# Expert 0's first product ahead of the routing, its rows from a slot table of twelve tiles, with a branch that does expert 0 again

## The chip, the core and the metric

The kernel runs on one core of a Trainium2 chip. The metric is the device time of one execution in microseconds (us). TensorE multiplies, VectorE and ScalarE work on vectors, GpSimd too (and it issues the gathers), SyncE issues most of the other transfers. In the profile they are PE (PEld is its loading of weights), DVE, ACT, POOL and SP.

## What is computed

Three stages in a row, each on 2304 tokens of 512 values; the last two have 8 experts with a hidden width of 1024.

```python
attn = softmax(q k^T / 8) v            # in chunks of 64 tokens, 8 heads of 64
# first mixture: one expert for each token, at most capacity = 576 tokens each
e = argmax(x @ w_gate);  g = softmax(x @ w_gate)[e]
out[i] = g[i] * relu(x[i] @ w1[e]) @ w2[e]       # by the order of the tokens in each expert
# second mixture: every expert for every token
P = exp(x @ w2_gate - max), 8 times: rows and columns divided by their sums, times N / E
out = sum over e of P[:, e] * relu(x @ w21[e]) @ w22[e]
```

The inputs are drawn from a fixed seed. Worked out with them, the reference sends 512, 128, 466, 384, 174, 128, 320 and 192 tokens to experts 0 to 7; of the first 1536 tokens (12 tiles of 128) 320 go to expert 0.

## The kernel before

A tile is 128 tokens; there are NT = 18. Numbers go as pairs of float16 (a high and a low part), so that a product is three matmuls: high by high, high by low, low by high.

**Attention and routing.** One loop over n (24 steps) runs the stages `st_...` of several tiles side by side, each with its lag, in the order written in `order`. `st_tr`, `st_dtr` and `st_xtr` transpose on TensorE through three PSUM banks (`ps_t`). The finished rows of a tile go to DRAM (`xs_d`) as a float16 pair by `st_hi` (ScalarE, L455) and `st_lo` (VectorE, L459, and the transfer). For each group of three tiles `route(g)` finds each token's expert and its place in it, and adds one product to a table in PSUM (`p_tab`, L570), from which `tacc` sums the table of slots: for expert e and slot s, the token's number (`gidx`, L577, after the last group). Expert 0's weights are loaded and split into pairs in the meantime. After the loop come the last group's steps, the table, and one matmul (L685) that counts the tokens of every expert, into the registers that branches and addresses read (`reg_i`, L686).

**The experts of the first mixture.** For expert x, GpSimd gathers rows of `xs_d` by the table (L712): slots 0 to 255 (`first`, for later experts `rows`) and 256 to 511 (`late`). Their transposes come from TensorE (`turn`) or from a transfer of SyncE (`turn_dma`, L721). The gathered tiles, like all tiles of this stage, take memory that the pools of the attention stage held until they were closed, behind the count. `blocks` does 256 tokens: a first product of four groups of 24 matmuls (L764), each followed by two vector steps (`hh` on ScalarE, L768; `hl` on VectorE, L769), then a second product of two times 24 (L781) with its scaling and two transfers. The first call is for everyone; if an expert has over 256 tokens, a second call on the `late` rows runs in a branch, for one or two tiles. Between the groups stand `sites`, the places where the next expert's weights are made ready: `w_scale`, then `w_split`, which makes the pairs. `behind`, after the first tile of the second product, holds the statistics (`w_stat`) of the expert after that: a sum of squares on ScalarE (L168) or a largest value on VectorE (L170). The loads go to SyncE in program order (L157).

**The rest.** The second mixture (from L910) is a long chain of products with every transfer planned by hand; the change doesn't touch it.

## Time and profile before

| | |
|---|---|
| median of 3 timed runs | 1789.73 us (1787.1 to 1792.47) |
| the profiled execution | 1782.29 us, of which the span of the profile is 1780.6 us |
| TensorE busy in the span | 1695.9 us (95%) |
| granted TensorE clock, mean | 0.985 of full speed |

The profile is that of one execution; its span runs from its first to its last record. A line of it gives the start in us from there, the duration, the engine, the line of the kernel, the operation and its operands, and in brackets how long the engine had been idle and what released it.

### The profile page before, as it was taken

The numbers are of one execution on the slowest core, as the hardware profiler recorded it, in microseconds if no ns is written. First come the engines' busy times: TensorE is split into PE (matmuls) and PEld (weight loads), VectorE is DVE, ScalarE is ACT, GpSimd is POOL, SyncE is SP. The second block draws the span as 40 slices with busy tenths as digits, with TensorE's granted clock in tenths as the row PEclk, the third lists the DMA queues.
The fourth block names the chain that finished last, engine by engine and source line by source line (L and its number), as shares of the span: only waits on it lengthen the run. The fifth ranks groups of instructions, "written<-read, shape, count | busy, mean of one in ns | idle before, by whom it ended". The sixth has DMA issues, their size and how long they took to land.

```text
span 1780.6 us, 32980 instructions
## 1 busy us (share of the span) xinstructions
PE 1695.9 (95%) x13011; PEld 1227.1 (69%) x13011; DVE 1202.5 (68%) x2340; ACT 954.4 (54%) x1806; POOL 731.8 (41%) x754
## 2 busy tenths in 40 slices
PE   7877999999999999999999999999999999999995
PEld 5765667566555577777777777777777777777774
DVE  4896556766476766686677767676866776675652
ACT  7965556675355454665355545455653664453440
POOL 1345335552021334444454344454533553443432
PEclk9997999999999999999999999999999999999998
DMA  9847678942534223241324224223323142231200
GB/s 240 211 155 214 148 199 178 247 127 85 145 102 147 89 105 130 64 168 53 124 83 152 104 91 151 104 84 110 138 77 131 63 172 87 86 125 65 96 36 36
DMA packets 140902, 219.15 MB, mean 123 GB/s; under 512 B 62880, under 2 KB 81392, under 8 KB 140720
## 3 DMA queue, kind: packets, MB, share of 16 engines
q1 hardware_dynamic: 133728, 198.92, 35.6%
q0 software_dynamic: 5360, 17.24, 3.5%
q8 instruction: 115, 1.88, 0.4%
q14 instruction: 67, 0.55, 0.1%
q10 hardware_dynamic: 1632, 0.56, 0.1%
HBM read 167.56 MB, written 41.91 MB: 118 GB/s over the span
## 4 chain that ended last, share of the span: by engine, by line
PE 68%; DVE 5%; ACT 2%; DMA 1%; issue 1%; POOLq 0%; ACTq 0%; DVEq 0%
PE p_m L1122 35%; PE p_m L1210 28%; PE p_m L1254 5%; DVE wall L290 3%; ACT wall L289 1%; DVE acc L1189 1%; DMA out_dram<-acc,rk 1%; DVE el L1130 0%; PE p_m L1010 0%; ACT eh L1127 0%; DMA wb_d<-wall 0%; DVE tq L1137 0%; ACT tq L1162 0%; DMA x_d<-row 0%; DVE tq L1140 0%
## 5 line engine op out<-in xcount | busy, mean ns | idle before, releaser
L1122 PE MATMUL p_m<-x,wall 128*128 128x384 f16 x4032 | 666.7, 326 | 5.6 <-ACT tq L1162 4.1
L1210 PE MATMUL p_m<-wall,eh 128*128 128x256 f16 x3528 | 580.4, 273 | 0.0
L1122 PEld LDWEIGHTS <-wall 128*128 128x128 f16 x4032 | 394.0, 98 | 263.0 <-issue 8.4
L1134 POOL TENSOR_TENSOR el<-tq,eh 128x384 f16<-128x384 f32 x336 | 344.4, 1053 | 558.9 <-ACT eh L1127 558.6
L1210 PE MATMUL p_m<-wall,el 128*128 128x256 f16 x1764 | 480.8, 273 | 0.3 <-DVE el L1130 0.3
L1127 ACT ACTIVATE eh<-tq 128x384 f16<-128x384 f32 x540 | 274.0, 522 | 190.6 <-DVE tq L1140 101.9
L1210 PEld LDWEIGHTS <-eh 128*128 128x128 f16 x3528 | 344.3, 98 | 44.3
L1189 DVE SCALAR_TENSOR_TENSOR acc<-p_m,cf,acc 128x256 f32<-128x256 f32 (+1 forms) x378 | 175.1, 521 | 128.0 <-PE p_m L1210 128.0
L1137 DVE TENSOR_TENSOR tq<-p_m,tq 128x384 f32<-128x384 f32 x288 | 158.5, 556 | 128.3 <-PE p_m L1122 127.3
L1210 PEld LDWEIGHTS <-el 128*128 128x128 f16 x1764 | 172.6, 98 | 20.5 <-DVE el L1130 0.6
L1130 DVE SCALAR_TENSOR_TENSOR el<-tq,eh 128x384 f16<-128x384 f32 x204 | 175.7, 863 | 10.0 <-ACT eh L1127 8.6
L1140 DVE SCALAR_TENSOR_TENSOR tq<-tq 128x384 f32<-128x384 f32 x252 | 133.2, 553 | 2.9
L764 PEld LDWEIGHTS <-wall 128*128 128x128 f16 x1152 | 106.5, 100 | 26.5 <-issue 10.2
L1162 ACT COPY tq<-p_m 128x384 f32<-128x384 f32 x96 | 45.6, 475 | 110.2 <-PE p_m L1122 107.8
L764 PE MATMUL p_p<-xT,wall 128*128 128x256 f16 x768 | 90.3, 279 | 7.5 <-DMA sta<-in_moe_w_dram 2.8
L1254 PE MATMUL p_m<-wall,eh 128*128 128x512 f16 x288 | 85.6, 379 | 0.0
L268 POOL TENSOR_TENSOR tq<-stb 128x256 f32<-128x256 f32 x56 | 48.9, 873 | 81.9 <-DVE wsumsq L184 58.9
L1175 ACT ACTIVATE tq<-tq 128x384 f32<-128x384 f32 x84 | 43.9, 523 | 70.1 <-DVE tq L1137 70.1
L289 ACT ACTIVATE wall<-stb,wsb 128x256 f16<-128x256 f32 (+1 forms) x56 | 31.3, 606 | 87.5 <-DMA wb_d<-wall 62.1
L268 POOL TENSOR_TENSOR tq<-sta 128x256 f32<-128x256 f32 x56 | 45.0, 804 | 72.9 <-DVE wall L290 43.4
L240 POOL TENSOR_SCALAR stb<-stb,wsb 128x1024 f32<-128x1024 f32 x16 | 53.7, 3358 | 46.7 <-DVE tq L1137 43.4
L290 DVE SCALAR_TENSOR_TENSOR wall<-stb,wsb,wall 128x256 f16<-128x256 f32 (+1 forms) x56 | 38.1, 690 | 51.4 <-ACT wall L289 48.7
(261 smaller groups left out, 2123.3 us busy)
## 6 DMA issues: line engine op xcount, KB each, us to landing
x<-xt_d SPq DMA_DIRECT2D x147, 384.0 KB, 3.6
sta<-in_moe_w_dram SPq DMA_DIRECT2D x18, 1024.0 KB, 6.7
stb<-in_moe_w_dram SPq DMA_DIRECT2D x18, 1024.0 KB, 9.0
wb_d<-wall SPq DMA_DIRECT2D x20, 896.0 KB, 3.6
wall<-wb_d SPq DMA_DIRECT2D x20, 896.0 KB, 6.3
sta<-in_moe_w_dram SPq DMA_DIRECT2D x28, 512.0 KB, 8.5
stb<-in_moe_w_dram SPq DMA_DIRECT2D x28, 512.0 KB, 6.3
xt_d<-x SPq DMA_DIRECT2D x21, 384.0 KB, 3.9
```

The costliest lines, as they stand in the source:

```text
L268: nc.gpsimd.tensor_tensor(out=at(o), in0=at(u), in1=at(v), op=op)
L290: nc.vector.scalar_tensor_tensor(out=o[:, cs, 1], in0=src, scalar=m.s, in1=o[:, cs, 0], op0=ALU.mult, op1=ALU.subtract)
L764: nc.tensor.matmul(p[:, f4, :], lhsT=w[:, kk, f * 128:(f + 1) * 128], rhs=xT[:, lo + kk, 0:W], start=(n == 0), stop=(n == 3 * KD - 1))
L1122: nc.tensor.matmul(p, lhsT=wt[:, w, lw, kk, :], rhs=xt[:, lx, kk, :], start=first and n == 0, stop=n == 5, skip_group_check=not first)
L1127: nc.scalar.activation(out=hs[op][0][:, q, :], in_=src, func=AF.Relu if op in (A11, A12, A22) or plain else AF.Copy)
L1130: nc.vector.scalar_tensor_tensor(out=hs[op][1][:, q, :], in0=src, scalar=0.0, in1=hs[op][0][:, q, :], op0=ALU.max, op1=ALU.subtract)
L1134: nc.gpsimd.tensor_tensor(out=hs[op][1][:, q, :], in0=src, in1=hs[op][0][:, q, :], op=ALU.subtract)
L1137: nc.vector.tensor_tensor(out=o, in0=a, in1=b, op=ALU.add)
L1140: nc.vector.scalar_tensor_tensor(out=o, in0=a, scalar=0.0, in1=b, op0=ALU.max, op1=op)
L1189: nc.vector.scalar_tensor_tensor(out=acc[:, j, cols], in0=y, scalar=coefs[x][:, j:j + 1], in1=acc[:, j, cols], op0=ALU.mult, op1=ALU.add)
L1210: nc.tensor.matmul(bk.t[:, cols], lhsT=hs[op][lh][:, q, t * 128:(t + 1) * 128], rhs=b.q[q][:, w, lw, :], start=m in (1, 5) and q == 0 and ...
L1254: nc.tensor.matmul(y.t, lhsT=h[:, kk % 4, c * 128:(c + 1) * 128], rhs=w[:, kk, :], start=(n == 0), stop=(n == 3 * KF - 1))
```

## The change

- **A slot table of twelve tiles.** The table of group 3 (tiles 9 to 11) is done in step 19 instead of 20 to 22 (`hooks`). From the sum over groups 0 to 3, VectorE takes expert 0's first 256 slots (`e_idx`), and GpSimd gathers those rows into the buffer of the weights (`wall`), which is free then. The number of expert 0's tokens in these tiles is kept in `e_count` a group later.
- **The first product of expert 0** moves into the end of the attention loop: the transposes after step 21 (`turn_into`), the groups of 24 matmuls after steps 22 and 23, after the last group's vector steps, and ahead of the count. The three transpose banks are shared with it.
- **Expert 1's statistics** are all sums of squares on ScalarE, three after step 22, three after step 23, two further on. Before, four were on VectorE.
- **Expert 1's splits of its first matrix** and the loads of expert 2 come ahead of expert 0's second product, the rest of the splits after its first tile. The transposes of the `late` rows come after both tiles.
- **The loads** of experts 2 and up are each preceded by a `memset` of one column on VectorE, on which the load then waits; from expert 1 on they are issued quarter by quarter in the sites.
- **A branch** behind expert 0: if the twelve tiles hold under 256 of its tokens, both tiles are done again from the whole table.

```diff
@@ -149,11 +149,13 @@
         m.src = src
         m.mx = smw("wmx" + nm, [128, 4])
 
-    def w_load(x, nm, h, nh=2):
+    def w_load(x, nm, h, nh=2, behind_vector=False):
         if h == 0:
             w_new(x, nm)
         m = mats[x, nm]
         c = m.kk // nh
+        if behind_vector:
+            nc.vector.memset(m.st[:, h * c, 0:1], 0.0)
         nc.sync.dma_start(out=m.st[:, h * c:(h + 1) * c, :],
                           in_=m.src[h * c * 128:(h + 1) * c * 128, :].rearrange("(k p) n -> p k n", p=128))
...
+    banks = {i: ctx.enter_context(tc.tile_pool(name="ps_a", bufs=1, space=PSUM)) for i in range(1)}
+    turns = {"p": [0, 1, 2], "y": [3, 4], "c": [5, 6]}
+
+    def bank_tile(i, shape, dtype, nm):
+        return banks[0 if i in (0, 1, 2) else 1].tile(shape, dtype, tag=f"m{i}", name=nm)
+
+    def in_turn(kind, shape, dtype, nm):
+        i = turns[kind].pop(0)
+        turns[kind].append(i)
+        return bank_tile(i, shape, dtype, nm)
+
+    early = wall[:, 2 * 4096:4 * 4096]
+    e_rows = [wall[:, t * 2 * XW:(t + 1) * 2 * XW].bitcast(F32) for t in range(2)]
+    e_hh, e_hl, e_xT = (early[:, i * 2048:(i + 1) * 2048].rearrange("p (k t) -> p k t", t=256) for i in range(3))
+    e_idx = const.tile([128, 2], I32, name="e_idx")
+    e_kg = const.tile([128, 2], F32, name="e_kg")
+    e_count = const.tile([128, 2], I32, name="e_count")
+    EG = NG - 3
+
+    def turn_into(xT, rows, bank):
+        for n, (idx, kg, xg) in enumerate(rows):
+            p = in_turn(bank, [128, 2 * KD, 128], F16, "p_t")
+            for kk in range(2 * KD):
+                nc.tensor.transpose(p[:, kk, :], xg[:, kk * 128:(kk + 1) * 128], id16)
+            sl = slice(n * 128, (n + 1) * 128)
+            nc.scalar.copy(out=xT[:, 0:KD, sl], in_=p[:, 0:KD])
+            nc.vector.tensor_copy(xT[:, KD:2 * KD, sl], p[:, KD:2 * KD])
+
+    def first_product(x, xT, hh, hl, W, bank):
+        a = mats[x, "a"]
+        FG = 512 // W
+        for fg in range(KF // FG):
+            p = bank([128, FG, W])
+            for f4 in range(FG):
+                f = fg * FG + f4
+                n = 0
+                for w, lo in ((a.hi, 0), (a.hi, KD), (a.lo, 0)):
+                    for kk in range(KD):
+                        nc.tensor.matmul(p[:, f4, :], lhsT=w[:, kk, f * 128:(f + 1) * 128], rhs=xT[:, lo + kk, 0:W],
+                                         start=(n == 0), stop=(n == 3 * KD - 1))
+                        n += 1
+
+            def hidden(fs=slice(fg * FG, fg * FG + FG), p=p):
+                nc.scalar.activation(out=hh[:, fs, :], in_=p, func=AF.Relu)
+                nc.vector.scalar_tensor_tensor(out=hl[:, fs, :], in0=p, scalar=0.0, in1=hh[:, fs, :],
+                                               op0=ALU.max, op1=ALU.subtract)
+
+            yield hidden
...
-                p = ps_t.tile([128, PR, 128], F32, tag="t", name="p_t")
+                p = in_turn("p", [128, PR, 128], F32, "p_t")
...
+        e_tokens = [(e_idx[:, j:j + 1], e_kg[:, j:j + 1], e_rows[j][:, 0:DM].bitcast(F16)) for j in range(2)]
+        e_first = first_product(0, e_xT, e_hh, e_hl, 256, lambda shape: in_turn("p", shape, F32, "p_p"))
+        hidden, hooks = [], {}
+        next_stats = [lambda nm=nm, h=h: w_stat(1, nm, h, True) for nm in "ab" for h in range(4)]
+
+        def early_gather():
+            nc.vector.tensor_copy(e_idx, tacc[:, 0:2])
+            for j in range(2):
+                nc.gpsimd.indirect_dma_start(out=e_rows[j], out_offset=None, in_=xs_d[0:(EG + 1) * G * 128, :],
+                                             in_offset=bass.IndirectOffsetOnAxis(ap=e_idx[:, j:j + 1], axis=0))
+
+        def counted():
+            nc.vector.tensor_copy(e_count, p_tab[:, 256:258])
+
         todo_r = {}
         for n in range(NT + 6):
             if n % 2 == 1 and n // 2 + 2 < NS:
@@ -650,8 +714,19 @@
                 for r in first + mm:
                     r()
             if i >= 0 and i % G == G - 1 and i < NT - G:
-                for m, part in zip((n, n + 1, n + 1, n + 3, n + 5), route(i // G)):
-                    todo_r.setdefault(m, []).append(part)
+                first_g, mm_g, mid_g, tab_g, last_g = route(i // G)
+                if i // G == EG:
+                    kept_g, sum_g, out_g = last_g
+                    hooks[n + 2, st_lo] = [kept_g, out_g]
+                    hooks[n + 2, st_scores] = tab_g
+                    hooks[n + 2, st_max] = [sum_g, early_gather]
+                else:
+                    todo_r.setdefault(n + 3, []).append(tab_g)
+                    todo_r.setdefault(n + 5, []).append(last_g)
+                if i // G == EG + 1:
+                    mid_g.append(counted)
+                todo_r.setdefault(n, []).append(first_g)
+                todo_r.setdefault(n + 1, []).extend((mm_g, mid_g))
...
+                for r in hooks.pop((n, f), ()):
+                    r()
...
+            if n == NT + 3:
+                turn_into(e_xT, e_tokens, "p")
+                for j in range(2):
+                    nc.vector.tensor_copy(e_kg[:, j:j + 1], e_rows[j][:, DM:DM + 1])
+            if n >= NT + 4:
+                hidden.append(next(e_first))
+                for f in next_stats[:3]:
+                    f()
+                next_stats = next_stats[3:]
         for n in sorted(todo_r):
             for part in todo_r[n]:
                 for r in part:
                     r()
-        for r in [gw, eps, rec, sel, pos, kx, rout, *second, *tab, tot1, tot2, racc]:
+        for r in [gw, eps, rec, sel, pos, kx, rout, *second]:
             r()
+        hidden.append(next(e_first))
+        hidden[0]()
+        for r in [*tab, tot1, tot2, racc]:
+            r()
+        next_stats[0]()
+        hidden[1]()
+        next_stats[1]()
+        hidden.append(next(e_first))
...
+        for f in hidden[2:]:
+            f()
...
+            if x == 0 and main:
+                hh, hl = e_hh, e_hl
+            else:
+                hh = cp.tile([128, KF, 256], F16, tag="hh", name="hh", bufs=1)[:, :, 0:W]
+                hl = cp.tile([128, KF, 256], F16, tag="hl", name="hl", bufs=1)[:, :, 0:W]
+                for hidden in first_product(x, xT, hh, hl, W, lambda shape: bank("p", shape)):
+                    hidden()
...
+        def load(x, nm, *hs):
+            return [lambda h=h: w_load(x, nm, h, 4, True) for h in hs]
...
-        first = gather(tokens(0, 0, 1))
+        pre = (None, e_tokens)
+
         late = gather(tokens(0, 2, 3))
         rows = gather(tokens(1, 0, 1))
-        for f in stats(1):
-            f()
-        pre = turn(first, "xT")
 
         for x in range(E):
             y = x + 1
-            rc = nc.values_load(reg_i[0:1, x:x + 1], min_val=0, max_val=N)
+
+            def count():
+                return nc.values_load(reg_i[0:1, x:x + 1], min_val=0, max_val=N)
+
+            if x > 0:
+                rc = count()
...
+            def rows_ahead():
+                return gather(tokens(y, 2, 3)) if y < E else None, gather(tokens(y + 1, 0, 1)) if y + 1 < E else None
+
             cur, pre = pre, turn_dma(rows) if y < E else None
-            late_cur, late = late, gather(tokens(y, 2, 3)) if y < E else None
-            rows = gather(tokens(y + 1, 0, 1)) if y + 1 < E else None
-            if x == 0:
-                for nm in "ab":
-                    loads(2, nm)
-            elif x + 2 < E:
-                loads(x + 2, "b", 0, 2)
+            late_cur = late
+            if x > 0:
+                late, rows = rows_ahead()
...
-                      ((0, "a"), (2, "b"), (1, "a"), (2, "a"), (3, "b"), (3, "a"), (0, "b"), (1, "b"))]
+                      (((0, "a"), (2, "b"), (1, "a"), (2, "a"), (3, "b"), (3, "a"), (0, "b"), (1, "b")) if x > 0 else
+                       ((0, "a"), (1, "a"), (2, "a"), (3, "a"), (2, "b"), (3, "b"), (0, "b"), (1, "b")))]
...
-            if 0 < x < E - 2:
-                sites[1].append(lambda: loads(x + 2, "b", 2, 4))
-            behind = [lambda: loads(x + 3, "a", 0, 2)] if x + 3 <= E else [lambda: loads(E, "b")] if x == E - 2 else []
+            later = load(x + 3, "a", 0, 1, 2, 3) if x + 3 <= E else load(E, "b", 0, 1, 2, 3) if x == E - 2 else []
+            behind = later[:1]
             for h in range(4):
                 if x + 2 <= E:
                     behind.append(lambda h=h: w_stat(x + 2, "a", h, True))
                 if x + 2 < E:
                     behind.append(lambda h=h: w_stat(x + 2, "b", h, False))
+                    if x > 0:
+                        sites[h] += load(x + 2, "b", h)
                 elif x == E - 1:
                     sites[h].append(lambda h=h: w_stat(E, "b", h, True))
-            sites += [behind, [lambda: loads(x + 3, "a", 2, 4)] if x + 3 <= E else []]
-            nxt = []
-            blocks(x, cur, 2, ranks(0), sites, True, lambda: nxt.append(turn(late_cur, "xTc", "p")))
+                if h in (1, 3):
+                    behind += later[h // 2 + 1:h // 2 + 2]
+            if x == 0:
+                def next_rows():
+                    ahead.append(rows_ahead())
+
+                ahead = []
+                every = [f for part in sites for f in part]
+                for f in load(2, "a", 0, 1, 2, 3) + load(2, "b", 0, 1, 2, 3) + every[:8]:
+                    f()
+                blocks(x, cur, 2, ranks(0), [[*every[8:], next_rows], []], True)
+                late, rows = ahead[0]
+                rc = count()
+                nxt = [turn(late_cur, "xTc", "p")]
+                for f in [*(f for f in behind if f not in later), *later]:
+                    f()
+                known = nc.values_load(e_count[0:1, 0:1], min_val=0, max_val=N)
+                with tc.If(known <= 255):
+                    for t in range(2):
+                        blocks(x, turn(gather(tokens(0, t), "xgl", 1), "xTl", "c"), 1, lambda _, t=t: ranks(0)(t))
+            else:
+                sites += [behind, later[3:]]
+                nxt = []
+                blocks(x, cur, 2, ranks(0), sites, True, lambda: nxt.append(turn(late_cur, "xTc", "p")))
```

## Rows read from the trace of the kernel before

**Rows 1.** The page, its first part: busy times, shares, instructions.

```profile
PE 1695.9 (95%) x13011; PEld 1227.1 (69%) x13011; DVE 1202.5 (68%) x2340; ACT 954.4 (54%) x1806; POOL 731.8 (41%) x754
```

**Rows 2.** Stretches: length, then PE, PEld, DVE, ACT, POOL busy, clock, DMA share, GB/s.

```profile
131.65:147.42 15.77, 3.66 (x33) 2.55 (x32) 12.01 (x41) 6.60 (x12) 8.77 (x12) 0.51 0.34 99
147.42:152.50 5.08, 5.08 (x25) 3.56 (x25) 0.41 (x1) 0.00 (x0) 3.86 (x5) 0.50 0.63 176
```

**Rows 3.** TensorE in order of time, from the last logits to expert 1.

```profile
130.59 1.06 PE L477 MATMUL p_lg<-g,xT 128*128 128x8 f32 x8 [0.92 <-ACT xT L471]
...
139.72 0.17 PE L685 MATMUL p_tab<-gohx,ones 128*128 128x16 f16 x1 [0.85 <-DVE gohx L684]
...
147.42 5.23 PE L764 MATMUL p_p<-xT,wall 128*128 128x256 f16 x24 [0.67 <-ACT xT L732]
...
172.17 10.64 PE L764 MATMUL p_p<-xTc,wall 128*128 128x256 f16 x96
194.28 2.78 PE L764 MATMUL p_p<-xT,wall 128*128 128x256 f16 x24 [1.10 <-PEq L899]
```

**Rows 4.** ScalarE in order of time.

```profile
131.74 0.72 ACT L455 ACTIVATE row<-x,x1s 128x512 f16<-128x512 f32 x1 [1.20 <-DVE x1s L90]
133.14 0.22 ACT L497 ACTIVATE gex<-gd 128x24 f32<-128x24 f32 x1 [0.68 <-DVE gd L495]
133.27 1.04 ACT L168 ACTIVATE wsq<-sta 128x1024 bf16<-128x1024 f32 x1
...
134.44 1.06 ACT L168 ACTIVATE wsq<-sta 128x1024 bf16<-128x1024 f32 x1
...
152.69 0.60 ACT L768 ACTIVATE hh<-p_p 128x512 f16<-128x512 f32 x1 [5.32 <-PE p_p L764]
```

**Rows 5.** VectorE in order of time: experts 0 and 1.

```profile
146.06 0.42 DVE L733 COPY xT<-p_t 128x512 f16<-128x512 f16 x1 [1.46 <-ACT xT L732]
...
163.71 0.68 DVE L769 SCALAR_TENSOR_TENSOR hl<-p_p,hh 128x512 f16<-128x512 f32 x1
...
169.80 4.94 DVE L170 TENSOR_REDUCE wmxb<-stb 128x1 f32<-128x1024 f32 x4
...
208.77 2.73 DVE L248 SCALAR_TENSOR_TENSOR wall<-stb,wsb,wall 128x1024 f16<-128x1024 f32 x2
...
214.38 4.59 DVE L170 TENSOR_REDUCE wmxb<-stb 128x1 f32<-128x1024 f32 x4
```

**Rows 6.** GpSimd in order of time.

```profile
120.51 0.81 POOL L599 DMA_DIRECT2D xs_d<-gkr  x1 [1.98 <-DVE gkr L598]
...
140.85 1.09 POOL L712 DMA_INDIRECT xg<-xs_d,gidx  x1 [2.42 <-PE p_tab L685]
...
143.51 0.95 POOL L712 DMA_INDIRECT xg<-xs_d,gidx  x1 [0.30 <-issue]
```

**Rows 7.** SyncE's transfers: start, time to issue.

```profile
150.05 5.08 SPq L721 DMA_TRANSPOSE xT<-xg  x2
155.43 1.98 SPq L157 DMA_DIRECT2D sta<-in_moe_w_dram  x4
...
200.59 4.07 SPq L721 DMA_TRANSPOSE xT<-xg  x2
```

**Rows 8.** Issue to landing, us: issued at 146.03, 161.5, 206.2 and 325.3.

```profile
xg<-xs_d,gidx POOLq DMA_INDIRECT x1, 3.9
...
stb<-in_moe_w_dram SPq DMA_DIRECT2D x1, 512.0 KB, 11.9
...
stb<-in_moe_w_dram SPq DMA_DIRECT2D x2, 512.0 KB, 6.1
...
sta<-in_moe_w_dram SPq DMA_DIRECT2D x2, 512.0 KB, 9.1
```

**Rows 9.** The stretch of expert 2's loads, columns as in group 2.

```profile
160.60:173.40 12.80, 12.75 (x79) 6.84 (x77) 11.27 (x16) 10.41 (x18) 9.61 (x6) 1.00 1.00 367
```

**Rows 10.** The start of expert 6 on TensorE.

```profile
347.68 4.11 PE L764 MATMUL p_p<-xT,wall 128*128 128x256 f16 x24 [2.85 <-DMA sta<-in_moe_w_dram]
```

More of the change, by code (lines that the diff above doesn't have):

```diff
@@ L702 @@
         second_of_odd.append(xw)
-        sums["bank"] = ps.tile([128, 512], F32, tag="l", name="p_sum")
+        sums["bank"] = banks[1].tile([128, 512], F32, tag="l", name="p_sum")
         for x in range(2, E + 1, 2):
@@ L1045 @@
     P = ep.tile([128, NT, E], F32, name="P")
-    p_lb = ps.tile([128, 512], F32, tag="l", name="p_l")
+    p_lb = banks[1].tile([128, 512], F32, tag="l", name="p_l")
     p_l = p_lb[:, 0:NT * 2 * E].rearrange("p (j c) -> p j c", c=2 * E)
```

48 lines of the change are left out of this document (7 added, 41 removed).

## The prediction

> **What bounds the kernel now.** The page comes first: TensorE is busy for 95% of the span [rows 1], so time can only be won where it stands still or runs slowly. Going through the stretches, the one large hole is between attention and expert 0. From the end of the last logits at 130.59 + 1.06 = 131.65 to expert 0's first product at 147.42, TensorE works 3.66 of 15.77 us; the granted clock falls to 0.51, and the first 24 matmuls then take 5.23 us at the lower of the two levels (1.2 GHz, row 0.50) against 2.78 us at 2.4 GHz [rows 2, 3]. The timelines show what fills the hole: VectorE finishes the last group's routing, TensorE counts at 139.72, and the first gather starts at 140.85, released by the count [rows 3, 6]. It isn't the table that releases it but the memory: the gathered rows lie where the attention pools lay, and the count is the last to read those.
>
> The next thing to see is what stands behind the gathers. SyncE begins the transposes of expert 1's rows at 150.05, as soon as the fifth gather has landed (issued at 146.03, 3.9 us), and only then, at 155.43, the eight loads of expert 2 [rows 7, 8]. The last of them goes out at 161.5 and lands 11.9 us later, at 173.4; VectorE's four statistics on them end at 169.80 + 4.94 = 174.74 [rows 5, 8]. In this kernel that hurts nobody: the `late` rows' first product has TensorE busy from 172.17, and expert 1 starts at 194.28 [rows 3].
>
> **The change, to the count.** The first twelve tiles hold 320 tokens of expert 0, more than the 256 that are gathered, so the branch that repeats expert 0 isn't entered. The rows: the transfer that completes group 3 follows that of 120.51 by some 1.5 us [rows 6]; with the gathers behind it, at about 125 and 126.3, and 3.9 us each [rows 8], the rows are there at 129 to 130.2, when TensorE comes to them. (A tile's transfer queued behind them on GpSimd goes out 1 us later; nobody reads it before 140.) In step 21 they put two copies of 0.42 us [rows 5] and small copies ahead of the last tile's scaling, and group 3's three steps are gone from there, so I put 1 us on it: ScalarE's row of the last tile ends at 131.74 + 0.72 + 1.0 = 133.4 [rows 4].
>
> Behind that row ScalarE now has six statistics, 1.17 us from start to start (133.27 to 134.44), with the exponential of 0.22 us between, and only then the first `hh` (0.60) [rows 4]: 133.4 + 7.0 + 0.2 + 0.6 = 141.3. VectorE's `hl` (0.68) ends at 142.0 [rows 5]. The fourth group of matmuls needs that bank and takes 2.7 us; the count, queued behind it on TensorE, is done at about 145.0 instead of 139.89 [rows 3]. That is 5.1 us later, and the table's last sum, which VectorE does behind the first `hl`, is later too.
>
> **From the count to expert 2's weights.** The gathers left are four. The third, the first of expert 1's, was issued 143.51 - 139.72 = 3.8 us behind the count [rows 3, 6]; now 148.8, landed at 152.7. The transposes then take 5.08 us, or 4.07 as at 200.59, where few gathers stand around them [rows 7]; the second is nearer. The loads start 0.3 us behind, at 157.1 (before: 155.43). The `memset`s that they also wait for follow the last `hl` at about 147 and are long done. Landing took 173.4 - 155.43 = 18.0 us; without the four gathers that move behind the splits (4 x 128 x 520 x 4 bytes = 1.06 MB, at the 367 GB/s of that stretch 2.9 us [rows 9]) 15.1 us: 172.2. Bounds: 157.1 + 4.2 MB / 367 GB/s = 168.5, and 158.1 + 18.0 = 176.1.
>
> **What waits for them.** A second product takes 194.28 - 1.10 - (172.17 + 10.64) = 10.4 us [rows 3]. Expert 0's began at 172.17 - 10.4 = 161.8; now it begins with the scale sums behind the count, at 145.6, and ends at 156. So TensorE is 16 us ahead there. Then it has nothing but the `late` rows. Their transposes now come last; ScalarE and VectorE have the four splits of expert 1's first matrix, both tiles' scaling and the other splits ahead of the copies, which I put at 164.5. And in program order the statistics of expert 2 stand ahead of the `late` rows' `hh` and `hl`. Two banks let TensorE do two of the four groups; then it waits for `hl`, that is for VectorE's fourth statistic on a quarter that lands at 172.2.
>
> The sum from there: a statistic 1.24 (a quarter of 4.94), the four `memset`s for the next loads 0.4 (each between nothing and the 0.42 of the copy), reading the register and going past the branch 1.1 (as the gap at 194.28; between nothing and the 2.85 at 347.68 [rows 3, 10]), `hl` 0.68: 175.6. Then two groups, 5.3, the second product, 10.4, and the gap of 1.1: expert 1 starts at 192.4 instead of 194.28, **1.9 us earlier**. With the bounds: 168.5 gives 188.3 by this path, where the other one (below) ends at 189.4, a gain of 4.9; 176.1 with the dear branch and `memset`s gives 199.4, a loss of 5.1. VectorE loses 4.6 us of statistics on expert 1 (a row like 214.38 [rows 5]), which nothing was waiting for. From expert 1 on the order is the old one but for eight small `memset`s an expert and the quarter loads; I cost both at nothing, covered by products of 10.4 us and more, and price the loss of that cover as a rival. Expert 1's splits on GpSimd, and the gathers for experts 1 and 2 behind them, end by about 174; SyncE and TensorE ask for them from 192 on. Behind expert 1 TensorE sets the pace, so the difference stays to the end.
>
> The profiled execution took 1782.29 us (span 1780.6 and 1.69 around it), 7.4 us under the median of the runs; I take the difference over to the median: 1789.73 - 1.9 = **1787.8 us**. About 0.3%, 5.4 us, is what a measurement of this kernel tells from no change.
>
> **Rivals.** *The weights don't hold the `late` rows (faster).* If the quarters land by 166, statistics at 164.5 to 169.2, branch and `hl` to 171 come in time. The `late` rows start at 164.5, 7.7 us ahead of 172.17, and the low clock after TensorE's idle 8 us takes 5.23 - 2.78 = 2.5 us back [rows 3]; with 189.4 for expert 1 it is 4.9 us, without the low clock 7.4: 1782.3 to 1784.8. For it: 367 GB/s for the late part of the loads. Against: the row of 18.0 us, and that the transposes come first.
>
> *Later loads hang on VectorE (slower).* For experts 1 to 5 the fourth quarter of the second matrix is issued only when VectorE has done the last split, at 208.77 + 2.73 = 211.5 in the trace of before, and its statistic is due at 214.38 + 3.4 = 217.8 [rows 5]. The decision lies at a landing time of 6.3 us: 6.1 was measured for two loads, 9.1 where more was in flight [rows 8]. At 9.1 VectorE stands 2.8 us in each of five experts, 14 us if none of it is hidden; with the 1.9 gained that is 1801.8, and with half of it hidden 1794.8. Against: TensorE has three banks and a second product to cover it.
>
> *The early gather is held up.* The Trainium skill (SBUF — State Buffer, "SBUF: two separate sides") states that a transfer issued from GpSimd can't have its descriptors written while VectorE runs one of its two-port operations; this speaks against gathering at 125, where VectorE is busy. By that rule the rows would come later by some operations of VectorE, and the trace shows no sign of it: GpSimd's transfer at 120.51, amid such work, took 0.81 us. Worked out from rows: the rows' slack ahead of TensorE is about nothing, so each us of delay moves the count and the sum by one; 5 us give 1792.8, still within 0.3%.
>
> *The change doesn't do what it says:* the branch is taken. Two blocks of a tile each cost at least half of the 21 us of 172.17 to 193.2 each: 1809. The reference's 320 tokens speak against it.
>
> **How the numbers follow.** Forecast 0.52, weights in time 0.25, later loads 0.18, gather 0.04, branch 0.01. The forecast's own range is 1784.8 to 1794.8. Same: 0.46 of the forecast, 0.07 of the weights' case, 0.02 of the loads', 0.03 of the gather's, 0.58; faster: 0.18 of the weights' case and 0.04 from the forecast's edge, 0.22; slower: 0.16, 0.02, 0.01 and 0.01, 0.20. The range 1781 to 1797 leaves out the dear end of the later loads and the branch.
>
> **What would show it.** In the changed profile TensorE should go from the logits into L764-like groups at 132 at the full clock, count near 145, gather third near 148.8, load expert 2 near 157, end VectorE's statistics near 173.5, and stand still in the middle of the `late` rows' first product. It is wrong if the loads land by 168 or the `late` rows start much ahead of 164, if the count comes before 142 or after 148, or if VectorE waits for quarters of experts 3 to 7.

## The result, and the profile after

The changed kernel takes 1800.64 us (median of 5 runs, 1797.4 to 1806.4) against 1789.73: a ratio of 1.0072, 95% interval 1.0044 to 1.0100. Run once more beside later experiments it had 1796.33 against 1788.74, 1.0047 (1.0026 to 1.0068). Its median is 8 to 11 us higher; forecast were 1787.8 us and no measurable difference, with a range to 1797. The two profiled executions (1797.4 and 1782.29 us) lie 15.1 us apart: that of before was 7.4 us under its median, that of the changed kernel 3.2.

The first view is TensorE's timeline of the changed kernel; its rows answer to [rows 3].

```profile
131.24 1.87 PE L331 MATMUL p_t<-id,wall 128*128 128x128 f16 x16
134.57 5.15 PE L346 MATMUL p_p<-wall 128*128 128x256 f16 x24
139.97 5.40 PE L346 MATMUL p_p<-wall 128*128 128x256 f16 x48
145.40 2.78 PE L346 MATMUL p_p<-wall 128*128 128x256 f16 x24
148.02 0.17 PE L779 MATMUL p_tab<-gohx,ones 128*128 128x16 f16 x1
149.01 10.52 PE L855 MATMUL p_y<-wall 128*128 128x512 f16 x48
159.37 1.06 PE L331 MATMUL p_t<-id,xg 128*128 128x128 f16 x16
179.01 12.97 PE L346 MATMUL p_p<-xTc,wall 128*128 128x256 f16 x96 [18.59 <-DVEq L983]
...
203.44 2.78 PE L346 MATMUL p_p<-xT,wall 128*128 128x256 f16 x24 [1.09 <-ACT sq L858]
```

The large hole has moved. Expert 0's first product now fills the time before the count, and its second product ends at 159.5 and the transposes of the `late` rows at 160.4, but then TensorE stands still from 160.43 to 179.01. What ends this wait is `DVEq L983`: the sequencer of VectorE, at the line of the redo branch. Not one of the four groups of the `late` rows runs before. Expert 1 starts at 203.44 instead of 194.28 [rows 3].

VectorE and SyncE show why VectorE comes to that line so late; these answer to [rows 5, 7].

```profile
156.06 3.62 SPq L811 DMA_TRANSPOSE xT<-xg  x2
160.04 3.69 SPq L159 DMA_DIRECT2D sta<-in_moe_w_dram  x4
163.77 2.13 SPq L159 DMA_DIRECT2D stb<-in_moe_w_dram  x4
```

```profile
171.91 3.84 DVE L172 TENSOR_REDUCE wmxb<-stb 128x1 f32<-128x1024 f32 x3 [4.60 <-DMA stb<-in_moe_w_dram]
177.50 1.22 DVE L172 TENSOR_REDUCE wmxb<-stb 128x1 f32<-128x1024 f32 x1 [1.75 <-DMA stb<-in_moe_w_dram]
```

In program order the branch stands behind the statistics of expert 2. The last of these waits for a quarter that lands at 177.50 and ends at 178.72, and 0.3 us later TensorE goes. The table by stretches of the changed kernel (columns as in [rows 2]) gives the price of the clock:

```profile
131.24:139.97 8.73, 8.73 (x62) 7.29 (x62) 4.40 (x19) 6.49 (x14) 1.91 (x3) 0.53 0.30 115
139.97:148.02 8.05, 8.05 (x79) 7.24 (x76) 5.32 (x24) 5.89 (x11) 2.18 (x3) 1.00 0.04 3
160.43:179.01 18.58, 0.00 (x0) 0.03 (x1) 11.07 (x17) 7.71 (x14) 12.96 (x8) 0.58 0.99 298
179.01:184.00 4.99, 4.99 (x25) 3.48 (x26) 0.00 (x0) 0.00 (x0) 0.18 (x1) 0.52 0.66 79
```

Twice TensorE works at 1.2 GHz (0.53, 0.52): in the first group, which takes 5.15 us instead of 2.78, and at the start behind the hole, where 96 matmuls take 12.97 us instead of 10.64 [rows 3]. Ahead of the second stretch it had stood still. Ahead of the first it had worked: it was busy for 4.39 of the 5.00 us from 124.00 to 129.00, at the full clock.

The second place is expert 5, where before had a gap of 0.44 us after 40 matmuls of the first product:

```profile
327.00 6.27 PE L764 MATMUL p_p<-xT,wall 128*128 128x256 f16 x56 [0.44 <-issue]
```

In the changed kernel, after 24 + 13 matmuls:

```profile
330.97 2.78 PE L346 MATMUL p_p<-xT,wall 128*128 128x256 f16 x24 [1.26 <-PEq L991]
333.58 0.28 PE L179 MATMUL p_sum<-wmxa,ones 128*128 128x4 f32 x2
333.73 0.36 PE L179 MATMUL p_sum<-wmxb,ones 128*128 128x4 f32 x2
333.95 1.58 PE L346 MATMUL p_p<-xT,wall 128*128 128x256 f16 x13
339.54 0.71 PE L346 MATMUL p_p<-xT,wall 128*128 128x256 f16 x5 [4.01 <-issue]
```

"Issue" means that the engine waited for nothing that the profile shows. The DMA queues of the half microsecond from 337.0 on (packets, MB, share) and of the whole execution have a candidate: the queue named instruction moves one packet while TensorE stands, and its packets are 1.92 MB / 117 = 16.4 KB each.

```profile
q1 hardware_dynamic: 54, 0.19, 95.2%
q8 instruction: 1, 0.02, 12.3%
```

```profile
q8 instruction: 117, 1.92, 0.5%
q14 instruction: 70, 0.57, 0.1%
```

A last 2.1 us go at the entry of the second mixture, where TensorE waits 2.64 us instead of 0.51 for a copy of ScalarE, which waits for a row that is written to DRAM (before, then after):

```profile
412.21 0.97 PE L1122 MATMUL p_m<-x,wall 128*128 128x384 f16 x5 [0.51 <-ACT x L1020]
426.64 0.80 PE L1217 MATMUL p_m<-x,wall 128*128 128x384 f16 x2 [2.64 <-ACT x L1115]
```

So of 15.1 us, 9.2 are there when expert 1 starts, 5.3 are added until the second mixture's first products (426.64 against 412.21), and 0.7 behind.

### The profile page after: what moved, and what is told of

It reads as the page before. It is cut to its first block, busy times and chain, and to the rows that moved or that the text cites. A ratio compares the mean times of both kernels' runs of the same rounds, so it can differ in the third digit from the quotient of the medians.

```text
span 1795.7 us, 33119 instructions
## 1 busy us (share of the span) xinstructions
PE 1703.5 (95%) x13011; PEld 1232.4 (69%) x13011; DVE 1198.5 (67%) x2395; ACT 959.3 (53%) x1814; POOL 729.7 (41%) x754
## 3 DMA queue, kind: packets, MB, share of 16 engines
q8 instruction: 117, 1.92, 0.5%
## 4 chain that ended last, share of the span: by engine, by line
PE 68%; DVE 5%; ACT 2%; DMA 1%; issue 0%; POOLq 0%; ACTq 0%; DVEq 0%
PE p_m L1217 35%; PE p_m L1305 28%; PE p_m L1349 5%; DVE wall L292 3%; DVE acc L1284 1%; ACT wall L291 1%; DMA out_dram<-acc,rk 1%; DVE el L1225 0%; PE p_m L1105 0%; ACT eh L1222 0%; DVE tq L1232 0%; DMA x_d<-row 0%; ACT tq L1257 0%; DVE tq L1235 0%; DVE wall L250 0%
## 5 line engine op out<-in xcount | busy, mean ns | idle before, releaser
L346 PE MATMUL p_p<-xT,wall 128*128 128x256 f16 x672 | 77.6, 276 | 10.3 <-issue 5.5
```

The lines of the kernel that those rows point to most:

```text
L346: nc.tensor.matmul(p[:, f4, :], lhsT=w[:, kk, f * 128:(f + 1) * 128], rhs=xT[:, lo + kk, 0:W], start=(n == 0), stop=(n == 3 * KD - 1))
```

## The experiments

Theory A: the skipped branch holds TensorE. The body of the redo uses the banks `c`, which the `late` rows use next; when it is skipped, that use counts as done for TensorE only once VectorE has itself come past the branch, and VectorE has the statistics and so the loads ahead of it. Rival B: the late loads alone, by way of `hl`. Rival C: the late count and the low clock. For the time behind expert 1, F: the quarter loads crowd TensorE's code; G: the added code shifts where its blocks end. Of the price of the branch, H says that it lies in the code of the body, which is jumped over, and I that it lies in having a branch there at all. "Gaps" is the sum of TensorE's waits without a releaser between 205 and 450 us in the profiled execution, and "late" and "x1" are the starts of the `late` rows' and expert 1's first products. Each kernel is compared with the kernel before on its own chip; the medians are of 10 runs, of 5 for the changed kernel, of 4 for e14 and e16.

| kernel | ratio to before, 95% interval | late | x1 | gaps |
|---|---|---|---|---|
| before | 1 | 172.17 | 194.28 | 2.5 |
| changed | 1.0072 (1.0044-1.0100) | 179.01 | 203.44 | 6.9 |
| changed, again (e9) | 1.0047 (1.0026-1.0068) | 176.98 | 201.47 | 7.1 |
| e1 branch first | 1.0026 (1.0004-1.0049) | 168.97 | 195.00 | 6.5 |
| e2 other banks | 1.0031 (1.0013-1.0049) | 167.88 | 196.51 | 7.1 |
| e3 statistics last | 1.0047 (1.0028-1.0066) | 167.28 | 191.98 | 11.9 |
| e4 loads first | 1.0024 (1.0004-1.0045) | 171.81 | 196.22 | 3.6 |
| e5 old loads | 1.0007 (0.9986-1.0028) | 178.94 | 202.77 | 7.5 |
| e6 before + quarter loads | 1.0025 (1.0003-1.0047) | 178.29 | 200.39 | 4.9 |
| e7 no branch | 0.9972 (0.9956-0.9988) | 166.76 | 192.34 | 3.1 |
| e8 four repairs | 1.0035 (1.0014-1.0056) | 173.49 | 197.96 | 6.1 |
| e10 small body | 1.0016 (0.9988-1.0044) | 169.33 | 194.75 | 5.2 |
| e11 loop body | 1.0047 (1.0022-1.0073) | 168.66 | 197.60 | 11.8 |
| e12 in order | 1.0018 (0.9995-1.0041) | 163.72 | 191.23 | 6.2 |
| e13 before + branch | 1.0020 (1.0009-1.0030) | 176.81 | 198.90 | 6.8 |
| e14 changed, code shifted 20 | 1.0117 (1.0096-1.0139) | 177.13 | 200.76 | 14.1 |
| e15 e1 with old loads | 0.9997 (0.9979-1.0016) | 166.91 | 192.88 | 6.6 |
| e16, e17, e18: e15 shifted 40, 64, 100 | 1.0072, 1.0054, 1.0054 | 168.37, 174.69, 169.68 | 197.72, 199.29, 194.44 | 7.6, 8.8, 15.9 |

The starts hold a part that is not the change's. VectorE's maximum of step 16 (L404, in the changed kernel L454), ahead of the steps that the change moves, comes at 102.31 us in the kernel before, at 102.86 and 104.69 in the two profiles of the changed kernel and at 105.78 in e12. So up to 3.5 us of a start lie there, and a start is best read with the wait ahead of it.

**e1, the branch ahead of the statistics.**

```diff
-                for f in [*(f for f in behind if f not in later), *later]:
-                    f()
                 known = nc.values_load(e_count[0:1, 0:1], min_val=0, max_val=N)
                 with tc.If(known <= 255):
...
+                for f in [*(f for f in behind if f not in later), *later]:
+                    f()
```

> One part moved: the redo branch stands ahead of expert 2's statistics in every engine's order instead of behind them. Theory A (the late rows' first product uses the two banks that the skipped branch also uses, so TensorE is let go only when VectorE's own sequencer has passed the branch, and VectorE has expert 2's statistics, which wait for the loads, ahead of it): TensorE starts the late rows' first product when their copies are ready and the branch is passed, about 168.5 instead of 179.0; it does two groups, waits for hl behind the statistics to about 179.5, and expert 1 starts at 196 to 197 instead of 203.4; the whole kernel 6 to 7 us under the changed kernel. Theory B (the late loads themselves, by way of hl alone; the branch adds nothing): TensorE still starts late, near 179, expert 1 near 203, no difference. Theory C (the late count and the low clock are the loss): no difference.

TensorE's timeline of e1:

```profile
168.97 7.97 PE L346 MATMUL p_p<-xTc,wall 128*128 128x256 f16 x48 [7.14 <-DVEq L981]
177.98 2.23 PE L346 MATMUL p_p<-xTc,wall 128*128 128x256 f16 x19 [1.04 <-DVE hl L352]
```

L981 is the branch there. The wait still ends with VectorE's passing, but now 10 us earlier; two groups run, and then the wait for `hl` is the one that the prediction had foreseen. Theory A holds; B and C fall as the whole cause (of B a wait of 1.04 us for `hl` is left).

**e2, other banks for the body.**

```diff
...
-                        blocks(x, turn(gather(tokens(0, t), "xgl", 1), "xTl", "c"), 1, lambda _, t=t: ranks(0)(t))
+                        blocks(x, turn(gather(tokens(0, t), "xgl", 1), "xTl", "y"), 1, lambda _, t=t: ranks(0)(t), kind="y")
```

> Order as in the changed kernel, but the branch's body uses the two banks of the second products (y) in place of those of the late rows (c). Theory A in its narrow form (what holds TensorE is the shared banks): the late rows' first two groups start near 168 again, expert 1 at 197 to 198, 5 to 7 us under the changed kernel. Theory A in its wide form (any skipped branch holds all engines until each has passed it): no difference, 179 and 203. Theory B: no difference.

```profile
167.88 6.82 PE L346 MATMUL p_p<-xTc,wall 128*128 128x256 f16 x48 [6.34 <-ACT xTc L333]
178.37 1.87 PE L346 MATMUL p_p<-xTc,wall 128*128 128x256 f16 x8 [3.67 <-DVE hl L352]
```

With the order of the changed kernel and nothing but other banks, the wait for a sequencer is gone: TensorE starts when its rows are copied. It is the shared bank that ties TensorE to VectorE, not the branch as such.

**e3, the statistics and what follows behind the `late` block; e4, expert 2's loads ahead of the transposes** (in e3 the loop of e1 moves behind the last `cmp.Else()` block of expert 0):

```diff
+            if x == 0:
+                for f in load(2, "a", 0, 1, 2, 3) + load(2, "b", 0, 1, 2, 3):
+                    f()
             cur, pre = pre, turn_dma(rows) if y < E else None
```

> Expert 2's statistics and the loads and memsets behind them stand behind the late rows' block, so neither the branch nor hl has them ahead. Theory A and theory B: the late rows start near 168.5 (copies ready at 167.3, branch passed), 10.6 us and some 2 us of low clock, second product 10.4, gap 1.1: expert 1 at 192 to 193 instead of 203.4; the kernel 9 to 11 us under the changed one, about level with the kernel before or 1 to 2 us under it. Theory C (late count, low clock): at most the restart's 2 us come back.

> Expert 2's eight loads are issued on SyncE ahead of the transposes of expert 1's rows. Theory A and theory B: the loads go out from about 150 instead of 160, the last of them lands 6 to 10 us earlier, VectorE's statistics end at 169 to 172 instead of 178.7, the late rows start at 170 to 173 and expert 1 at 194 to 197; 6 to 9 us under the changed kernel. If the loads are not what the statistics wait for (theory C): no difference. A possible loss: the transposes, now behind the loads, are late for expert 1; they have until 194.

```profile
191.98 2.78 PE L346 MATMUL p_p<-xT,wall 128*128 128x256 f16 x24 [1.11 <-ACT sq L858]
197.94 0.39 PE L179 MATMUL p_sum<-wmxa,ones 128*128 128x4 f32 x2 [3.17 <-ACT wsq L170]
```

```profile
171.81 1.44 PE L346 MATMUL p_p<-xTc,wall 128*128 128x256 f16 x6 [11.76 <-DVEq L986]
```

In e3 expert 1 starts 2.3 us before the kernel before, and then meets the statistics that were put off (3.17 us) and more gaps, so its time, expected level with before, was missed by 8 us. In e4 the hold ends when the earlier loads have landed, 7 us sooner, as foretold: the hold lasts as long as the loads do. In all five profiles with the hold (changed, e4, e5, e9, e14) TensorE starts 0.3 us after VectorE's last statistic ends.

**e5 to e8.** e5 gives experts 1 to 6 their old loads; e6 puts the quarter loads into the kernel before; e7 has no branch; e8 joins e4, e5 and a new order, whose core is the last line.

```diff
             if x > 0:
                 late, rows = rows_ahead()
+                if x + 2 < E:
+                    old_loads(x + 2, "b", 0, 1)
...
-                    if x > 0:
-                        sites[h] += load(x + 2, "b", h)
...
+                    sites[1].append(lambda: old_loads(x + 2, "b", 2, 3))
...
+                blocks(x, cur, 2, ranks(0), [[lambda: nxt.append(turn(late_cur, "xTc", "p")), *every[8:], next_rows], []], True)
```

> The changed kernel with the weight loads of experts 1 to 6 issued as before (half a matrix at a time, no memset of VectorE ahead, the second matrix's first half straight behind the transposes); the start, the branch and expert 2's loads stay as changed. Expert 1 still starts near 203.4. Theory F (the quarter loads leave 1.5 MB instead of 1 MB in flight when an expert begins, and the block of TensorE's code that its first product needs lands behind them: the gap without a visible releaser in expert 5's first product, 4.01 us in the changed kernel and 4.6, 6.0, 4.8 and 1.9 in the four runs so far): that gap falls to at most 1 us as before, and the time is 3 to 5 us under the changed kernel. Theory G (the added branch shifts the code, and the gap lies where a block of code happens to end): the gap stays at 4 to 6 us and the time stays.

> The kernel before with this one part of the change: from expert 1 on the loads go out in quarters behind VectorE's memsets, at the changed places. Expert 1 starts at 194 to 195 as before. Theory F: a gap of 4 to 6 us opens in expert 5's first product and the time is 3 to 6 us above the kernel before. Theory G: no gap over 1 us, no difference.

> The changed kernel without the redo branch (the repeat of expert 0 for a short list is left out). Theory A: TensorE starts the late rows when their copies are ready, 166 to 168, does two groups and waits for hl to about 179; expert 1 at 195 to 197 instead of 203.4, as with the other banks. Theory B: 179 and 203. For the gap in expert 5: theory F keeps it at 2 to 6 us, theory G moves it or takes it away, as the code is shorter by the branch's body.

> Four repairs together: expert 2's loads ahead of the transposes; the late rows' transposes and copies between expert 0's two second products, ahead of the splits; the branch ahead of VectorE's statistics, and those behind the late rows' block (ScalarE's stay ahead); the loads of experts 1 to 6 as before. Theory A with F: TensorE goes from expert 0's second product (end near 160.5) past the branch at about 162 into the late rows without a hole of more than 2 us, at the full clock; expert 1 starts at 184 to 187, no gap over 1.5 us in expert 5, and the time is 6 to 10 us under the kernel before. If only the late rows' copies or the splits are moved from one queue to the other, expert 1 starts at 190 to 194 and the time is that of the kernel before.

TensorE's timeline of e6 (expert 5, after its 40th matmul), and of e8:

```profile
336.21 1.20 PE L766 MATMUL p_p<-xT,wall 128*128 128x256 f16 x6 [3.73 <-issue]
```

```profile
158.55 1.03 PE L331 MATMUL p_t<-id,xg 128*128 128x128 f16 x8 [2.99 <-DMA xg<-xs_d,gidx]
173.49 1.87 PE L346 MATMUL p_p<-xTc,wall 128*128 128x256 f16 x8 [7.81 <-ACTq L997]
```

The quarter loads, with their `memset`s and their places, make the kernel before 4.5 us slower (1.0025), and the gap at the 40th matmul opens from 0.44 to 3.73 us: F speaks. (Its expert 1 starts 6.1 us after that of [rows 3], though nothing is changed up to there: so much do single executions differ.) But with the branch in the code, e5 has 2.37 us in expert 5 and 4.43 in expert 7, where the changed kernel had 1.13, and e7's gap is only 1.92 with the quarter loads: G speaks too. e8 was my mistake by theory A itself: it left ScalarE's statistics ahead of the branch, and the wait ends with ScalarE's sequencer at the branch (L997), while the loads put ahead made the `late` rows land later.

**e9 to e12.** e9 is the changed kernel; e10 cuts the body (first diff); e11 makes it a loop (second); e12 joins that, e8's last line, e5 and e3, and puts expert 1's scale sums a group later.

```diff
                 with tc.If(known <= 255):
-                    for t in range(2):
-                        blocks(x, turn(gather(tokens(0, t), "xgl", 1), "xTl", "c"), 1, lambda _, t=t: ranks(0)(t))
+                    nc.vector.memset(cp.tile([128, 1], I32, tag="idx", name="idx"), 0)
```

```diff
+                    with tc.For_i(0, 2, 1) as t:
...
+                        blocks(x, turn(gather([idx], "xgl", 1), "xTl", "y"), 1, lambda _: rank(t), kind="y")
```

> The changed kernel once more, unaltered, as the yardstick on the chip of the next three: 1.005 to 1.009 of the kernel before. TensorE held at the redo branch from about 160 to 179; expert 1 at 201 to 205. Gaps without a visible releaser in the first products of experts 5 to 7, 4 to 8 us together; whether they stand at the same places as in the first profile (expert 5) tells whether they belong to the code's layout or to the moment.

> The changed kernel with the redo branch kept but its body cut to one small memset of VectorE (the repeat of expert 0 is left out). Theory A: no bank is shared with the body any more, TensorE starts the late rows at 166 to 168 and expert 1 at 192 to 197. Theory H (the code of the body, which every engine jumps over, is what costs beyond the hold: the kernel without a branch had 0.9972 of before, the one with other banks 1.0031): the time is like that without a branch, 0.996 to 0.999. Theory I (having a branch there costs, whatever is in it): 1.001 to 1.005, as with the other banks.

> The changed kernel with the redo written as a loop over the two tiles, half the code, and on the second products' banks (y). Theory A: expert 1 at 195 to 198. Theory H: between the other banks (1.0031) and the small body, 0.998 to 1.002. Theory I: 1.001 to 1.005.

> A version meant to have the early start without the hold: redo as a loop on the banks y straight behind expert 0's second product; the late rows' transposes and copies between its two tiles, ahead of the splits; expert 2's loads behind the transposes as changed; its statistics behind the late block; expert 1's scale sums one group of matmuls later, so that TensorE does not meet those statistics; loads of experts 1 to 6 as before. Theory A: the late rows start at 161 to 163, two groups, then wait for hh and hl behind the splits to 167 to 169, expert 1 at 184 to 188, 7 to 10 us ahead of the kernel before; with at most 5 us of gaps more than before, 0.994 to 0.999. If TensorE is held at 166 or later by a sequencer or by the copies, expert 1 is at 190 or later and the time 1.000 or more.

TensorE's timeline of e10 (first line) and of e12:

```profile
169.33 6.94 PE L346 MATMUL p_p<-xTc,wall 128*128 128x256 f16 x48 [6.33 <-ACT xTc L333]
163.72 5.41 PE L346 MATMUL p_p<-xTc,wall 128*128 128x256 f16 x48 [0.45 <-PEq L991]
172.38 3.90 PE L346 MATMUL p_p<-xTc,wall 128*128 128x256 f16 x20 [3.25 <-DVE hl L352]
```

e10 stands 6.2 us under e9 (1790.13 and 1796.33 on one chip, with intervals that overlap), with a branch but no shared bank. H and I aren't told apart: e10's interval holds the values of both, and e11, at half the code, is no better than the full body. e9's gap in expert 5 (3.69 us) lies after the 37th matmul as in the first profile, so it belongs to the code. In e12 the `late` rows start at 163.7 without a hole and at the full clock, and then wait 3.25 us for `hl`, which is behind the splits. Expert 1 comes at 191.2, not at 184 to 188; but this execution was 3.5 us late in step 16 already, and less that difference it would be 187.8 (an estimate).

**e13 to e15, what is left behind expert 1.** e13 adds the skipped branch (e2's, at `rc <= 255`) to the kernel before; e14 is

```diff
                 nxt = [turn(late_cur, "xTc", "p")]
+                for _ in range(20):
+                    nc.tensor.matmul(sums["bank"][:, 256:384], lhsT=id16, rhs=id16)
```

and e15 is e1 with the loads of e5.

> The kernel before with the redo branch alone, skipped, between expert 0's block and its late rows, on the banks y. Theory A: no bank of the late rows is shared, expert 1 at 194 to 197. Theory I (a branch costs where it stands): 1 to 2 us more, 1.000 to 1.002. Theory G (the added code moves the place at which TensorE's next block of code is needed into a crowded moment): the gap in expert 5 stands after the 37th matmul of its first product instead of the 40th, as in all runs with the full body, and grows from 0.44 to 2 to 5 us although the loads are as before; time 1.001 to 1.004. Theory F alone (quarter loads): the gap stays under 1 us.

> The changed kernel with 20 small matmuls of the identity in TensorE's hole at 160 to 179 (their result is not used), so that all later code of TensorE lies 20 matmuls further on. Theories F and G (the gap in expert 5 is the wait for a block of TensorE's code): the gap moves from the 37th matmul of expert 5's first product (the 41st, with the four for the scale sums) to the 21st, inside the first group of 24, and stays at 3 to 5 us or grows, as the block is asked for 4 us earlier beside the loads. If the gap belongs to data (weights, rows, a bank) it stays after the 37th. Expert 1 and the time as in the changed kernel, 1.003 to 1.008 of before.

> Two repairs of the changed kernel alone: the redo branch ahead of expert 2's statistics, and the loads of experts 1 to 6 as before. If the hold at the branch (6 to 8 us) and the quarter loads (2 to 4 us) are the whole of the loss: expert 1 at 194 to 197, the gap in expert 5 at 0.4 to 2.5 us, the time 0.998 to 1.001 of before. If the loss behind expert 1 does not hang on the loads: 1.002 to 1.004, as with the branch first alone (1.0026).

TensorE's timeline of e14, expert 5, and of e13, the `late` rows of expert 0 and of expert 7:

```profile
333.90 2.45 PE L346 MATMUL p_p<-xT,wall 128*128 128x256 f16 x21 [0.79 <-PEq L993]
341.55 0.80 PE L346 MATMUL p_p<-xT,wall 128*128 128x256 f16 x3 [5.20 <-issue]
```

```profile
176.81 10.65 PE L764 MATMUL p_p<-xTc,wall 128*128 128x256 f16 x96 [1.69 <-PEq L897]
...
381.65 1.65 PE L764 MATMUL p_p<-xTc,wall 128*128 128x128 f16 x14 [4.40 <-issue]
```

With 20 matmuls more ahead, the gap stands 20 matmuls earlier in expert 5 (after the 21st, where it was the 37th and four scale sums), as expected to the matmul: it goes with the place in the code and not with any data. Counted from the start of the execution, 2372 matmuls stand ahead of it in the changed kernel, e1, e3, e4, e5, e8, e9, e14 (its 20 among them) and e15 alike; only its length differs, from 1.7 to 5.2 us. And in each of the 34 gaps of 2 us and more between 150 and 450 us, over all profiles, a packet of the instruction queue ends 1.0 to 2.3 us ahead of TensorE's restart. So it is the wait for a block of TensorE's code. The Trainium skill (Runtime: NRT & Kernel Launch, Instruction fetch mechanics) says that an engine's code comes in blocks of 16 KiB by its own DMA queue, and that crossing into a block is mostly hidden. The packets of 16.4 KB agree; the hiding does not here: 4.0 to 6.0 us of gap in expert 5 in the changed kernel, e1, e2 and e3. In e13 the loads are as before and the branch is skipped. TensorE waits 1.69 us for its own sequencer at the line of the branch (L897), where before it had no wait, and the gaps are 6.8 us instead of 2.5 (1.62 in expert 5, 4.40 in expert 7); the time is 1.0020. So part of the price is theory I's. As for G, the branch moves the gap in expert 5 by three matmuls only, from the 40th to the 37th, and why it is longer there isn't shown. e15 comes to 0.9997, and expert 1 to 192.88.

**e16 to e18** are e15 with 40, 64 and 100 small matmuls of 64 columns at the place of e14's.

> The two repairs (branch first, loads as before; 0.9997 of before) with 40 small matmuls of the identity in TensorE's hole before the late rows (result not used), which push all later code of TensorE 40 matmuls on. The gap in expert 5 moves from the 37th matmul of its first product (the 41st with the scale sums) to its start, where TensorE waits for the branch anyway; the one in expert 7's late rows (4.60 us) moves 40 matmuls forward too. If the code's place alone decides: gaps without a releaser behind expert 1 at 3 to 5 us together instead of 6.6, time 0.997 to 0.999. If no place is better than another: 0.999 to 1.002. A shift that hits worse, as the 20 matmuls did on the changed kernel (14.1 us of gaps): 1.003 or more.

> The same with 64 matmuls, half a block of TensorE's code (256 instructions, 128 matmuls with their weight loads, as the packets of some 16.4 KB in the row of the instruction queue have it): the block of expert 5 ends in the late rows' transposes, behind its first product (the 105th). Place decides: gaps at 2 to 5 us together, 0.996 to 0.999; no place better: 0.999 to 1.002.

> The same with 100 matmuls: the block ends after some 65 matmuls of expert 5's first product, 28 later than now, so it is asked for 3 us later. Place decides: less beside the loads issued behind the expert before, gaps at 2 to 5 us together, 0.996 to 0.999; no place better: 0.999 to 1.002. The late rows may start up to 1 us later, as 100 matmuls take 5 to 7 us of the hole of 7.

```profile
160.07 1.33 PE L992 MATMUL p_sum<-id 128*128 128x64 f16 x40
168.37 4.86 PE L346 MATMUL p_p<-xTc,wall 128*128 128x256 f16 x24 [6.96 <-ACT wsq L170]
...
197.72 2.50 PE L346 MATMUL p_p<-xT,wall 128*128 128x256 f16 x11 [5.49 <-issue]
```

In e16's timeline the 40 matmuls take 1.33 us of a hole, and yet it is 1.0072. The gap in expert 5 is gone, as expected, but others have opened: 5.49 us at the start of expert 1 (ahead of 205 us, so not in the table's sum), 4.45 and 3.15 us in expert 3. In e17 one lies in the hole ahead of the `late` rows: their last copy ends at 167.72, the code's packet at 173.44, and TensorE starts at 174.69, after a wait of 12.01 us for which the profile shows no releaser. All three are slower by 0.5 to 0.7%, above what was expected of e17 and e18. No place that was tried is better than the unshifted one, and no complete kernel was measurably faster than the one before; only e7 was, which leaves the redo out.

## Why the prediction was wrong

**The count.** The working took ScalarE's statistics and the first `hl` for what the fourth group waits for, and came to 145.0. It was 148.02, at its own bound. The first group began at 134.57 and ran at 1.2 GHz; from there on TensorE worked without a wait, and the fourth group at 145.40 followed directly on TensorE's own work. The statistics cost the count nothing: the first `hl` ended at 144.2, 2.2 us later than said, and still 1.2 us before the fourth group began. The terms left out were the low clock, 2.4 us, and a start 2.6 us later than the 132 that was said, 0.5 of it from the execution itself (step 16).

**The loads.** From the count on the steps hold: third gather 3.7 us behind it (3.8), loads 12.0 us behind it (12.1). The last landing came 17.5 us after the first issue, within the bounds of 11.4 and 18.0, but not at 15.1: taking the four gathers away brought hardly anything (18.0 before). Landing was 177.5 instead of 172.2, 3.0 of it from the count.

**The step that failed** is "Two banks let TensorE do two of the four groups; then it waits for `hl`". TensorE did none, since the skipped branch holds the banks. From landing to TensorE's start it took 1.5 us where 3.4 were said up to `hl`; but then four groups were to do, not two, 5.3 us more, at the low clock for 2.3 us more. 192.4 + 5.3 (landing) - 1.9 + 5.3 + 2.3 = 203.4, the measured start. That the hold is what TensorE waits for is shown by e1, e2 and e10, and its length by e4. In the profiles TensorE's hole there is 14.7 to 18.6 us with it (changed, e5, e9, e14) and 6.3 to 7.1 without (e1 to e3, e7, e10). What the hold costs in the whole time is less sure: 6 us in the medians of e9 and e10, some 2 between e5 and e15, and nothing between e9 and e11, where other gaps make up for it (11.8 us); the intervals overlap in all three pairs. The branch was costed as a read and a jump, 1.1 us (e13 shows 1.69); what stood in its body was not looked at for what it shares.

**Behind expert 1** the prediction said that the difference stays, and costed `memset`s and quarter loads at nothing, which failed too. In fact the quarter loads cost 4.5 us in e6, and 5 between e1 and e15 (1.0026 and 0.9997), so the rival of the later loads had the right part and the right sign. But its mechanism, VectorE waiting for late quarters, is not seen: its waits for the second matrix behind expert 1 are 1.0 us in all, as before. In e6 the 3.3 us of gap in TensorE's code show in its place; in the kernels with the branch, the old loads only move gaps from expert 5 to expert 7, so that there the way in which the loads cost time stays open. The skipped branch alone costs 3.6 us in e13 (1.6 to 5.4 by its interval). Of this the prediction had the wait at the branch, but no step of it had gaps in TensorE's code.

**What held.** The gather wasn't held up: it went out at 126.6 instead of 125, its two transfers took 1.04 and 0.97 us to issue, and TensorE didn't wait for its rows (in e3 and e14 it did, 2.0 and 2.2 us). The sign that the prediction gave for this was thin, as VectorE worked beside the transfer of 120.51 only up to 120.88, and no run varies VectorE's work beside the gather. The branch wasn't taken. And with both costs repaired (e15) expert 1 starts at 192.88, where 192.4 was forecast, two groups run, and the third waits for `hl` as foretold (0.88 us). The time is that of the kernel before; that the branch (3.6 us in e13) takes away the 1.9 us foretold, and more, is argued from e13 and not measured in e15. In the rival of the weights the sum is 0.3 us off: 164.5 + 13.1 + 10.4 + 1.1 = 189.1, a gain of 5.2 and not 4.9.

Open are the share of H and I in the branch, why the gaps are longer in one kernel than in another at the same place, and whether another place of the code would bring e15 under the kernel before.

## What to carry to other kernels

A branch that is skipped can still tie engines together: here the two banks that its body would have used were free for TensorE only when VectorE had come past the branch, with all that it had ahead in its order (e1, e2, e10). So put such a branch ahead of work that waits for transfers, or give its body banks of its own. And where 0.3% is at stake, compare with a version that only shifts the code: 20 matmuls that nobody needed cost about half a per cent here (e14, four runs). A start in one profile is no measure of a few us either, if the executions differ by as much ahead of the change.

## What the runs showed of the hardware that was not expected

TensorE's code arrives in packets of 16.4 KB beside the bulk loads, and where one is late TensorE stands for up to 6 us, in e17 for 7. Its gaps without a releaser behind expert 1 are 2.5 us in all in the kernel before, 3.1 to 15.9 in the others. The place goes with the count of instructions, to the matmul. TensorE's restart at 1.2 GHz behind a hole of 6 to 19 us costs 1.4 to 2.8 us (48 matmuls in 6.8 to 8.2 us instead of 5.4, 96 in 12.97 instead of 10.64). And executions of one program differ: the kernel before took from 1780.6 to 1801.9 us over all its runs, on several chips.
